# Two layers of linear attention and MLP on one core: another order for the first loads, two dummy matmuls less, and the instruction lists settled anew

## The chip, the core and the metric

The kernel runs on one core of a Trainium2 chip. A core has TensorE (PE) for matmuls, VectorE (DVE), ScalarE (ACT) and GpSimd (POOL) for elementwise work, and SyncE (SP), which only issues transfers. Each engine runs its own list of instructions strictly in order; semaphores order one engine against another. PSUM has eight banks, into which TensorE writes; a bank is free again when another engine has read it. The metric is the time of one execution in microseconds (us) on the device.

## The reference

Input x is 2048 tokens of 512 features in bf16. Four residual blocks follow one another: attention, MLP, attention, MLP, with the same weights in both layers.

```python
def _A_ref(x, wqkv, wo):                       # H = 32 heads of 16
    q, k, v = split_heads(x @ wqkv)
    phi = lambda t: jnp.where(t > 0, t + 1, jnp.exp(t)) + 1e-6
    pq, pk = phi(q), phi(k)
    kv = jnp.einsum("bhsd,bhse->bhde", pk, v)
    z = jnp.einsum("bhsd->bhd", pk)
    o = jnp.einsum("bhqd,bhde->bhqe", pq, kv) / (jnp.einsum("bhqd,bhd->bhq", pq, z)[..., None] + 1e-6)
    return merge_heads(o) @ wo
def _B_ref(x, w1, b1, w2, b2):                 # F = 1792
    h = _gelu(jnp.einsum("bsd,df->bsf", _layernorm(x), w1) + b1)
    return jnp.einsum("bsf,fd->bsd", h, w2) + b2
for _ in range(2):
    x = x + _A_ref(_layernorm(x), A_wqkv, A_wo)
    x = x + _B_ref(_layernorm(x), B_w1, B_b1, B_w2, B_b2)
```

The sums kv and z run over all tokens, so each attention block has a point at which every token's keys must be done before any output can start.

## The kernel before

The 2048 tokens are 16 tiles of 128 (numbered 0 to 15), in four chunks of four. Names in the kernel carry the layer and the tile or chunk: K0_3 is the key matmul of layer 0, tile 3; Q0_1_2 the query matmul of layer 0, chunk 1, part 2.

A tile of the first attention goes through these steps. VectorE takes its statistics (statsA0, line 773, and aggrA0, line 775), VectorE or POOL adds epsilon (vepsA0, line 780), POOL takes the power -1/2 (powA0, line 782), and VectorE normalizes (normA0, line 795); or POOL makes a bias (nmr, line 787) and ScalarE normalizes (line 790). Tile 3 alone has its statistics on ScalarE: a sum (line 764), a negation on POOL (negA0_3, line 766) and a sum of squares (line 768). Tiles 0 to 5 are then transposed on TensorE (PTA0, line 817) and copied out of PSUM by ScalarE (tcA0, line 827); the others are transposed by transfers that SP issues (TA0, line 804). K (line 866) multiplies a transposed tile by the key weights; ScalarE takes exp (line 837) and, for some, relu (line 848), and VectorE or POOL makes phi of it (min at lines 841 and 850, phik at lines 843 and 854). G (line 958) adds up the product of phi(k) with the normalized tile over all 16 tiles in four PSUM banks that stay held until G0_15; Z (line 941) adds up phi(k). Q (lines 883 and 896) makes the queries. After G0_15 and the Zs come kv (line 1008), its product with wo (line 1031), the denominators (D, line 1074, or per token on VectorE and POOL with TP transposes on SP, lines 1051 to 1063), and the attention output WO (line 1097). The MLP is W1 (line 1127), gelu on ScalarE (line 1132), and W2 (line 1163).

All order is written out by hand in one table, CONF. CONF["ORDER"] has one list of operation names for each engine; CONF["PLACES"] gives every buffer slot (PSUM banks, the 12 large SBUF slots t4, the small ones) the list of tiles that hold it one after the other; CONF["WAY"] names the engine of each operation that can run on more than one. Settled (line 105) takes these lists as they are, and assign_waits (line 186) adds semaphore waits for data and for slots that are still in use. An operation whose data is late therefore holds up everything behind it in its engine's list.

CONF["WARM"] gives two groups of dummy matmuls, warm0 and warm1 (line 747), on a constant; all write the bank "warm". CONF["LOADS"] lists the first transfers: name, queue, what, chunk, from and to tile of the chunk (or row block of the weights), and what it waits for. x0 and x1 are the tiles of chunk 0, wk0 and wk1 two halves of the key weights, xc1 to xc3 the other chunks, wq the query weights. The remaining weights (wv, wo, w1, w2) are issued by POOL after all transposes of the first attention (late, line 725). POOL also prepares constants: the identity (idp), a block mask (bdm0, bdm1, lines 729 and 732), eps6, and zeros for the bias transfer (b1z, line 723), behind which SP's b1 and its transpose Tb1 wait.

In ORDER, SP begins with x0, x1, wk0; ScalarE with wk1, xc1, xc3, sumA0_3, wq, sqA0_3, tcA0_0; TensorE with warm0, warm1, PTA0_0, PTA0_1, K0_0.

Of the kernel before, what the change touches and what calls it, by code (L numbers as in the profile page):

```python
# [185 lines left out]
def assign_waits(graph, order, sems, dma_sems):  # L186
# [10 lines left out]
    while len(done) < total:  # L197
        moved = False
        for e in ENGINES:
# [42 lines left out]
    WARM=[[512, 512, 512, 512, 512, 512, 512, 512, 512, 512, 512], [512, 512, 512, 512]],  # L242
    LOADS=[['x0', 'sp', 'x', 0, 0, 1, ''], ['x1', 'sp', 'x', 0, 1, 4, ''], ['wk0', 'sp', 'wk', 0, 0, 2, ''], ['wk1', 'act', 'wk', 0, 2, 4, 'ones'], ['xc1', 'act', 'x', 1, 0, 4, 'x0'], ['xc3', 'act', 'x', 3, 0, 4, ''], ['wq', 'act', 'wq', 0, 0, 4, ''], ['xc2', 'act', 'x', 2, 0, 4, '']],
    ORDER={
# [38 lines left out]
        "act":  # L283
# [321 lines left out]
def build_kernel(nc, A_x, A_wqkv, A_wo, B_x, B_w1, B_b1, B_w2, B_b2, out, conf=None, report=False):  # L605
# [5 lines left out]
    with ExitStack() as es:  # L611
# [131 lines left out]

        for n, cols in enumerate(cf["WARM"]):
            def warm(e, cols=cols):
# [584 lines left out]
```

## Time and profile before

| what | value |
|---|---|
| runs | 327.53, 329.68 and 484.78 us; median 329.68 |
| profiled execution: its own time | 327.5 us |
| its span, first to last instruction | 326.3 us |
| TensorE busy | 322.2 us in 1723 matmuls |
| VectorE, ScalarE, POOL busy | 211.0, 193.1, 152.5 us |
| x0, 128 KB: issue to landing | 2.4 us |
| x1, 384 KB: issue to landing | 3.1 us |
| wk0 and wk1, 256 KB each: issue to landing | 4.5 and 4.0 us |

The profile gives for one execution the busy time of each engine, the chain of work that ended last (each instruction followed back to what released it), groups of instructions by source line, a timeline, and busy times by stretch of the span. Times within it count from the first instruction. A busy TensorE is not TensorE at its peak: matmul ends are modelled, and the distance between two starts tells the rate. In a timeline line the start comes first, then the duration, engine, line, operation, output and inputs, and in brackets the idle time before it with what ended it.

### The profile page before, as it was taken

How to read it: one execution, taken by the hardware profiler on the slowest of the kernel's cores; microseconds unless marked ns; L12 is line 12 of the kernel's file. 1: busy time of each engine (PE TensorE's matmuls, PEld its weight loads, DVE VectorE, ACT ScalarE, POOL GpSimd, SP SyncE). 2: the span in 40 equal slices, each digit the busy share in tenths (PEclk: the TensorE clock that was granted, in tenths of full speed). 3: DMA queues.
4: the chain of work that ended last, by engine and by line, in shares of the span. 5: the costliest groups of instructions: out<-in, count | busy, mean ns of one | idle time of the engine just before them, and what ended most of it. 6: DMA issues, size and time to landing. Idle time of an engine off the chain costs nothing.

```text
span 326.3 us, 4763 instructions
## 1 busy us (share of the span) xinstructions
PE 322.2 (99%) x1723; PEld 159.3 (49%) x1723; DVE 211.0 (65%) x503; ACT 193.1 (59%) x334; POOL 152.5 (47%) x224
## 2 busy tenths in 40 slices
PE   8999999999999999999999999999999999999997
PEld 3444445576454444444444444458644444444444
DVE  5987679996938685142436899999989983300112
ACT  4988769797661416529673477969833454551600
POOL 5662548588663417300757434783856593100000
PEclk9999999999999999999999999999999999999999
DMA  7355753334012210331011110012034322200102
GB/s 266 120 83 97 219 189 104 105 64 68 16 32 50 54 26 3 80 64 34 0 32 33 34 32 0 19 32 50 17 82 94 69 48 66 64 0 2 64 0 80
DMA packets 46883, 20.37 MB, mean 62 GB/s; under 512 B 41932, under 2 KB 45388, under 8 KB 46860
## 3 DMA queue, kind: packets, MB, share of 16 engines
q1 hardware_dynamic: 44572, 13.00, 18.8%
q0 software_dynamic: 1056, 4.72, 4.5%
q10 hardware_dynamic: 1232, 2.36, 2.0%
q8 instruction: 13, 0.21, 0.3%
q14 instruction: 10, 0.08, 0.1%
HBM read 8.00 MB, written 2.10 MB: 31 GB/s over the span
## 4 chain that ended last, share of the span: by engine, by line
PE 97%; DVE 1%; ACT 1%; issue 0%
PE ps L1127 30%; PE ps L1163 29%; PE ps L1097 9%; PE ps L866 8%; PE ps L883 5%; PE ps L987 4%; PE ps L958 4%; PE ps L896 2%; PE ps L747 2%; PE ps L1150 1%; PE ps L1074 1%; PE ps L1008 1%; PE ps L1031 1%; PE ps L941 1%; PE ps L817 0%; DVE pkb L854 0%
## 5 line engine op out<-in xcount | busy, mean ns | idle before, releaser
L1132 ACT ACTIVATE gT<-ps,b1c 128x512 bf16<-128x512 f32 (+1 forms) x140 | 77.1, 600 | 65.3 <-PE ps L1127 65.0
L1127 PE MATMUL ps<-t,w 128*128 128x512 bf16 (+1 forms) x560 | 102.2, 336 | 0.0
L1163 PE MATMUL ps<-w,gT 128*128 128x512 bf16 x434 | 97.6, 379 | 0.0
L1127 PEld LDWEIGHTS ps<-t,w 128*128 128x128 bf16 x560 | 54.6, 98 | 43.7 <-ACT t L827 0.3
L1163 PEld LDWEIGHTS ps<-w,gT 128*128 128x128 bf16 x434 | 42.5, 98 | 50.4 <-DVE xsb L1169 0.2
L782 POOL TENSOR_TENSOR rstd<-veps,neghalf 128x1 f32<-128x1 f32 x64 | 37.9, 602 | 33.5 <-DVE veps L780 31.4
L837 ACT ACTIVATE eb<-ps 128x512 bf16<-128x512 f32 x64 | 37.4, 614 | 18.3 <-PE ps L866 10.5
L1173 DVE TENSOR_TENSOR outb<-ps,xsb 128x512 bf16<-128x512 f32 x15 | 10.1, 686 | 46.3 <-PE ps L1163 40.3
L773 DVE BATCH_NORM_STATS2 stats<-xsb 128x6 f32<-128x512 f32 x48 | 32.3, 678 | 0.4
L848 ACT ACTIVATE rb<-ps 128x512 bf16<-128x512 f32 x45 | 26.6, 617 | 9.2 <-PE ps L866 8.7
L866 PE MATMUL ps<-wqkv,t 128*128 128x512 bf16 x128 | 31.6, 379 | 0.1
L1097 PE MATMUL ps<-gtb,t 128*128 128x512 bf16 x128 | 31.2, 379 | 0.1
L850 DVE TENSOR_SCALAR eb<-eb 128x512 bf16<-128x512 bf16 x45 | 14.0, 321 | 21.1 <-ACT eb L837 21.1
L1113 POOL TENSOR_TENSOR xsb<-xsb,b2b 128x512 f32<-128x512 f32 x20 | 24.3, 1224 | 6.8 <-ACT yb L790 6.6
L790 ACT ACTIVATE yb<-xsb,nmr,rstd 128x512 bf16<-128x512 f32 x21 | 16.7, 812 | 14.2 <-POOL nmr L787 13.9
L780 POOL TENSOR_SCALAR veps<-mv 128x1 f32<-128x1 f32 x35 | 7.6, 217 | 30.8 <-DVE mv L775 28.1
L1063 POOL TENSOR_TENSOR t<-t,rr 128x512 bf16<-128x512 bf16 x14 | 15.5, 1114 | 13.6 <-DVE rr L1059 12.9
L795 DVE TENSOR_SCALAR yb<-xsb,mv,rstd 128x512 bf16<-128x512 f32 x27 | 16.1, 602 | 8.5 <-POOL rstd L782 8.3
L1051 POOL TENSOR_TENSOR lr<-t,zrow 128x512 f32<-128x512 bf16 x15 | 17.9, 1191 | 5.7 <-ACT zrow L971 4.2
L883 PE MATMUL ps<-wqkv,t 128*128 128x512 bf16 x80 | 19.9, 379 | 0.0
L1097 PEld LDWEIGHTS ps<-gtb,t 128*128 128x128 bf16 x128 | 12.3, 98 | 14.7 <-DVE rr L1059 0.6
L866 PEld LDWEIGHTS ps<-wqkv,t 128*128 128x128 bf16 x128 | 12.0, 98 | 14.9 <-ACT t L827 1.0
(97 smaller groups left out, 373.5 us busy)
## 6 DMA issues: line engine op xcount, KB each, us to landing
w<-in_B_w_dram POOLq DMA_DIRECT2D x4, 896.0 KB, 6.9
out_dram<-outb SPq DMA_DIRECT2D x15, 128.0 KB, 1.9
t<-in_A_x_dram ACTq DMA_DIRECT2D x3, 512.0 KB, 4.6
t<-yb SPq DMA_TRANSPOSE x56, 2.5
wqkv<-in_A_wqkv_dram ACTq DMA_DIRECT2D x1, 512.0 KB, 5.8
wqkv<-in_A_wqkv_dram POOLq DMA_DIRECT2D x1, 512.0 KB, 4.6
wo<-in_A_wo_dram POOLq DMA_DIRECT2D x1, 512.0 KB, 5.5
t<-in_A_x_dram SPq DMA_DIRECT2D x1, 384.0 KB, 3.1
```

The lines of the kernel that those rows point to most:

```text
L773: G.op("dve", lambda e: e.bn_stats(stats[:, s.slot, :], src()), 620, reads=src_keys, writes=[k + "s"], tiles=[s, *src_tiles], name=f"stats ...
L782: G.op("pool", lambda e: e.tensor_tensor(rstd[:, s.slot:s.slot + 1], veps[:, s.slot:s.slot + 1], neghalf[:], op=ALU.pow), 570, reads=[k + ...
L837: G.op("act", lambda e: e.activation(eb[:, et.slot, :], bank(bt), ACT.Exp), 478, reads=[src_key], writes=[f"e{tag}"], tiles=[bt, et], name ...
L848: G.op("act", lambda e: e.activation(rb[:, rt.slot, :], bank(bt), ACT.Relu), 478, reads=[src_key], writes=[f"r{tag}"], tiles=[bt, rt], nam ...
L866: ins = e.matmul(bank(b), lhsT=yTa(yT)[:, dt, k * P:(k + 1) * P], rhs=wqkv[:, dt, D:2 * D], start=(dt == 0), stop=(dt == DT - 1))
L883: ins = e.matmul(bank(b), lhsT=yTa(yT)[:, dt, k * P:(k + 1) * P], rhs=wqkv[:, dt, 0:D], start=(dt == 0), stop=(dt == DT - 1))
L1051: lambda e, r=r, tok=tok: e.tensor_tensor(lr[:, r.slot, :], tok(), zrow[:], op=ALU.mult), 1150 if on_pool else 600,
L1097: ins = e.matmul(bank(wb), lhsT=yTa(pq)[:, kt, k * P:(k + 1) * P], rhs=gtb[:, kt, :], start=(kt == 0), stop=(kt == DT - 1))
L1113: G.op("pool" if on_pool else "dve", lambda e: e.tensor_tensor(xsb[:, st, :], xsb[:, st, :], b2b[:], op=ALU.add), 1120 if on_pool else 600 ...
L1127: ins = e.matmul(bank(b, n), lhsT=w1[:, dt, ft * P:(ft + 1) * P], rhs=yTa(yT)[:, dt, k0 * P:k1 * P], start=(dt == 0), stop=(dt == DT - 1))
L1132: G.op("act", lambda e, ft=ft, b=b, k0=k0, k1=k1, n=n: e.activation(gT[:, g.slot, ft * 512 + k0 * P:ft * 512 + k1 * P], bank(b, n), ACT.Ge ...
L1163: ins = e.matmul(bank(b), lhsT=gT[:, g.slot, ft * 512 + k * P:ft * 512 + (k + 1) * P], rhs=w2[:, ft, :], start=(ft == 0), stop=(ft == FT - 1))
```

## The change

Only CONF changes; the functions stay as they are.

- WARM: warm1 has two dummies instead of four. In TensorE's list PTA0_0 now stands between warm0 and warm1.
- LOADS: x1, now tile 1 alone, is issued by ScalarE as its first instruction. The two halves of the key weights follow, wk0 as SP's second and wk1 as ScalarE's second, which no longer waits for the memset "ones". x2, tiles 2 and 3, is ScalarE's third. Then xc1 (still behind the landing of x0), xc3, wq and xc2, all ahead of ScalarE's first arithmetic.
- ORDER: all five lists are settled anew. PLACES follows them.
- WAY: 34 operations move from POOL to VectorE and 29 from VectorE to POOL (epsilons, denominator products pz and pr, bias additions b2, sums za). POOL's bdm0, bdm1, eps6 and b1z move from the start of its list to the place where the late weights are issued.

The diff, cut to its core (the lists that are left out change in the same way):

```diff
 CONF = dict(
-    WARM=[[512, 512, 512, 512, 512, 512, 512, 512, 512, 512, 512], [512, 512, 512, 512]],
-    LOADS=[['x0', 'sp', 'x', 0, 0, 1, ''], ['x1', 'sp', 'x', 0, 1, 4, ''], ['wk0', 'sp', 'wk', 0, 0, 2, ''], ['wk1', 'act', 'wk', 0, 2, 4, 'ones'], ['xc1', 'act', 'x', 1, 0, 4, 'x0'], ['xc3', 'act', 'x', 3, 0, 4, ''], ['wq', 'act', 'wq', 0, 0, 4, ''], ['xc2', 'act', 'x', 2, 0, 4, '']],
+    WARM=[[512, 512, 512, 512, 512, 512, 512, 512, 512, 512, 512], [512, 512]],
+    LOADS=[['x0', 'sp', 'x', 0, 0, 1, ''], ['x1', 'act', 'x', 0, 1, 2, ''], ['wk0', 'sp', 'wk', 0, 0, 2, ''], ['wk1', 'act', 'wk', 0, 2, 4, ''], ['x2', 'act', 'x', 0, 2, 4, ''], ['xc1', 'act', 'x', 1, 0, 4, 'x0'], ['xc3', 'act', 'x', 3, 0, 4, ''], ['wq', 'act', 'wq', 0, 0, 4, ''], ['xc2', 'act', 'x', 2, 0, 4, '']],
...
         "sp":
-            "x0 x1 wk0 TA0_7 TA0_6 TA0_8 TA0_14 TA0_15 TA0_13 TA0_12 b2 TA0_10 TA0_11 TA0_9 b1 Tb1 TB0_1 TB0_0
+            "x0 wk0 TA0_6 TA0_8 TA0_7 TA0_14 TA0_15 TA0_13 b2 TA0_12 TA0_10 TA0_11 TA0_9 b1 Tb1 TB0_1 TB0_0
...
         "pe":
-            "warm0 warm1 PTA0_0 PTA0_1 K0_0 PTA0_2 K0_1 PTA0_3 K0_2 PTA0_4 G0_0_0 K0_3 K0_4 Q0_0_0 G0_1_0 PTA0_5 Q0_0_1 K0_5
+            "warm0 PTA0_0 warm1 PTA0_1 K0_0 PTA0_2 K0_1 PTA0_3 K0_2 PTA0_4 G0_0_0 K0_3 K0_4 PTA0_5 G0_1_0 Q0_0_0 Q0_0_1
...
-            Q0_1_3 Q0_1_1 Q0_0_3 Q0_0_2 G0_8_0 Z0_3 Z0_2 G0_9_0 G0_10_0 D0_0_0
+            Q0_1_3 Q0_1_1 Q0_0_3 G0_8_0 Q0_0_2 Z0_3 Z0_2 G0_9_0 G0_10_0 D0_0_0
...
         "act":
-            "wk1 xc1 xc3 sumA0_3 wq sqA0_3 tcA0_0 xc2 tcA0_1 expk0_0 tcA0_2 reluk0_0 tcA0_3
+            "x1 wk1 x2 xc1 xc3 wq xc2 tcA0_0 sumA0_3 tcA0_1 sqA0_3 expk0_0 tcA0_2 reluk0_0 reluk0_1 expk0_1 tcA0_3
...
         "dve":
-            "ones statsA0_0 aggrA0_0 vepsA0_0 normA0_0 statsA0_1 aggrA0_1 vepsA0_1 statsA0_2 aggrA0_2 normA0_1 statsA0_4
-            aggrA0_4 normA0_2 statsA0_5 normA0_3 statsA0_7 mink0_0 normA0_4 phik0_0
+            "ones statsA0_0 aggrA0_0 statsA0_1 aggrA0_1 vepsA0_1 normA0_0 normA0_1 statsA0_2 aggrA0_2 vepsA0_2 statsA0_4
+            normA0_2 statsA0_6 aggrA0_4 mink0_0 normA0_3 statsA0_5 normA0_4 phik0_0
...
-            phik0_9 phik0_13 mink0_11 minq0_0_3 phik0_11 minq0_1_3 minq0_0_2 zs0_2 zs0_3 zb0
+            phik0_9 phik0_13 mink0_11 phik0_11 minq0_0_3 minq0_1_3 phiq0_1_3 zs0_2 zs0_3 zb0
...
         "pool":
-            "id0 eps6 bdm0 bdm1 neghalf id1 powA0_0 negA0_3 b1z powA0_1 vepsA0_2 powA0_2 vepsA0_3 powA0_3
+            "id0 id1 neghalf vepsA0_0 powA0_0 powA0_1 negA0_3 powA0_2 vepsA0_3 powA0_3
...
-            powA0_9 nmrA0_11 wv wo w1_0 w1_1 phik0_14 phiq0_1_1 w2_0
+            powA0_9 bdm0 eps6 wv bdm1 wo phik0_14 w1_0 phiq0_1_1 w1_1 pr0_0_2 w2_0 b1z
```

In layer 1 the new VectorE list has rec1_3_3 ahead of RB1_1 (before: behind RB1_2).

472 rows, old and new, of tables (ORDER, PLACES, WAY) are left out of this document.

## The prediction

> **What bounds the kernel now.** I read first the page's span, busy times and chain by engine, to learn whether there is anything to win outside TensorE.
>
> ```profile
> span 326.3 us, 4763 instructions
> ...
> PE 322.2 (99%) x1723; PEld 159.3 (49%) x1723; DVE 211.0 (65%) x503; ACT 193.1 (59%) x334; POOL 152.5 (47%) x224
> ...
> PE 97%; DVE 1%; ACT 1%; issue 0%
> ```
>
> TensorE stands idle 326.3 - 322.2 = 4.1 us in all. The change removes no real matmul. So its whole reach is two dummies and whatever part of the idle time is a wait, and I looked for those in the chain in order of time.
>
> ```profile
> 0.84 6.34 PE ps L747 x15
> 7.17 0.24 PE ps L817 x4
> 7.43 0.60 ACT t L827
> 8.09 1.04 PE ps L866 x4
> ...
> 38.54 0.60 ACT eb L837
> 39.16 0.29 DVE eb L841
> 39.45 0.34 DVE pkb L854
> 39.84 0.55 PE ps L941 x16
> ...
> 250.42 0.13 issue
> ```
>
> The reader sees 15 dummies (L747), then a short detour over ScalarE, then TensorE without a break except near 39 us and 250 us. A dummy takes 6.34 / 15 = 0.423 us, while real matmuls of the same width are 0.86 / 4 = 0.216 us apart: until about 6.8 us the array runs at half speed (the clock column says 1.00 throughout, and does not show this).
>
> Third, the busy time by stretch, for who paces TensorE behind the dummies:
>
> ```profile
> 7.00:9.00 2.00, 1.71 (x14) 0.88 (x13) 1.93 (x7) 1.18 (x2) 1.50 (x5) 1.00 1.02 382
> 9.00:11.00 2.00, 2.00 (x17) 1.14 (x16) 1.99 (x6) 1.84 (x4) 0.88 (x3) 1.00 0.96 319
> ...
> 35.00:40.00 5.00, 4.34 (x40) 2.09 (x38) 3.60 (x7) 3.22 (x7) 2.69 (x4) 1.00 0.99 295
> ```
>
> After the stretch and its length come the busy times of TensorE, its weight loads, VectorE, ScalarE and POOL. VectorE has 1.93 and 1.99 of 2.00; it is full from 5 to 20 us, so at the start it is as much the bound as TensorE. From 35 to 40 us nobody is full: there TensorE waits on a chain. Fourth, VectorE's own timeline:
>
> ```profile
> 4.99 0.41 DVE L795 TENSOR_SCALAR yb<-t,mv,rstd 128x512 bf16<-128x512 bf16 x1 [0.68 <-POOL rstd L782]
> 5.32 0.69 DVE L773 BATCH_NORM_STATS2 stats<-t 128x6 f32<-128x512 bf16 x1
> ...
> 7.14 0.38 DVE L795 TENSOR_SCALAR yb<-t,mv,rstd 128x512 bf16<-128x512 bf16 x1
> ...
> 8.34 0.38 DVE L795 TENSOR_SCALAR yb<-t,mv,rstd 128x512 bf16<-128x512 bf16 x1
> ...
> 39.16 0.29 DVE L841 TENSOR_SCALAR eb<-eb 128x512 bf16<-128x512 bf16 x1 [0.95 <-ACT eb L837]
> ```
>
> Tiles 0, 1 and 2 are normalized at 5.40, 7.52 and 8.72.
>
> **The dummies and the first tiles.** Two dummies less is 2 x 0.427 = 0.85 us off TensorE's list. What of it stays is a walk with the rows' durations (a VectorE instruction that does not read the one before it starts some 0.08 early). Tile 1 now has 128 KB of its own, first on ScalarE's queue. ScalarE issued at 1.49 in the middle of its table load (0.79 to 2.07), so the load does not hold it: I take issue at 0.85 and 2.4 us as for tile 0, landing 3.3; VectorE reaches it at 4.04. Were it issued only at 2.07, it would land at 4.46 and cost 0.4. VectorE: statistics of tile 0 at 3.21, of tile 1 at 4.04, normalize tile 0 at 5.1 (its rstd is ready at 5.05) and tile 1 at 5.84 to 6.24. TensorE: 11 dummies end at 5.53, the four transposes of tile 0 at half speed (0.107 each) end at 5.98, two dummies at 6.82, transposes of tile 1 at 7.05; tcA0_0 on ScalarE is over at 6.8, the key weights are there at 6.2 as before or sooner (the same 1 MB is in flight; its last part landed 4.5 us after its issue at 1.72; SP now issues its key weights at 1.26 and ScalarE its own no longer behind the ones at 1.49). So K0_0 starts at **7.05 instead of 8.09**, a whole microsecond early.
>
> What is late next is tile 2. Tiles 2 and 3 are now the last of that 1 MB, about 6.2 (4.4 before); statistics of tile 2 start at 6.2, before at 6.33. Tile 3's sum on ScalarE, at 4.42 before, now stands behind tcA0_0: 6.66 to 7.39. On POOL negA0_3 (0.26) waits for it until 7.47, and **powA0_2 is queued behind negA0_3**: 7.76 to 8.33. Tile 2 is normalized at 8.40 to 8.78, no sooner than before (8.72). K0_0 ends at 7.91 and TensorE waits 0.9. Then the same way tile 3 at 10.05 (9.64), tile 4 at 10.98 (10.76), phik0_0 at 11.31 (11.19), and G0_0_0 starts at 11.4, exactly as before. The same set of work up to Q0_0_1 ends at 16.8 against 16.93. So the start gives **-0.1**, of bounds -0.85 (no wait takes the place) and +0.7 (tiles 2 and 3 landing only at 7.5, when the load behind them did: issued 3.21, 4.3 us; tile 2 is then ready at 9.6 instead of 8.8). That load, tiles 4 to 7, is read at 7.5 as before.
>
> On the Trainium skill. The row: half speed lasted 6.0 us of unbroken dummies. "TensorE: Matmul & The Clock Gate", Part 1, says that the warm-up is about 3.4 us of sustained activity in a free-running window, not a number of matmuls. By it the opening stays where it is and the sum with it. Its Part 4 says that transposes do not count as busy in the same way; by that a window with tile 0's transposes in it may fail, and the opening come 3.4 us later, an estimate of +0.5 us from that page. The slower rival below is the same mechanism with its length from rows.
>
> **The wait near 39 us.** In the chain, phik0_11 (L854, 39.45) is followed by Z0_2 (L941). On VectorE mink0_11 is over at 38.21, but the list has minq0_0_3 before phik0_11, and that waits 0.95 us for an exponential of Q (L837). In the new list phik0_11 comes right behind mink0_11: 38.25 to 38.7. Z0_3 lets TensorE go at 39.02, so the gap of 39.84 - 39.02 goes: **-0.8**. Next is zb0 for D0_0_0; its chain starts from Z0_2 and moves with it, and VectorE has 1.4 of 5 us free. Bounds: -0.9 (a gap of 0.1 before Q0_0_2 goes too, which now stands behind G0_8_0) and 0.
>
> **The wait at 250 us.** WO1_15_0 waits for TP1_3_3, issued at 248.0 behind rec1_3_3 at 246.5, which stood behind RB1_2. Now rec1_3_3 stands ahead of RB1_1, some 5 us sooner: **-0.3**, bounds 0 and -0.3.
>
> **Costed at nothing.** 34 operations go from POOL to VectorE and 29 back. In 215 to 240 us VectorE is busy 23.6 of 25.0; four come (0.8 + 1.0 + 1.0 + 0.74), three go (3 x 0.74), a net +1.3 that fills it. Cover: W11_1 starts at 245.1, a microsecond after its last transpose; without it up to +1.3. POOL's bdm0, eps6 go ahead of wv, where it idles 6.3 us; bdm1 (0.85) and phik0_14 (1.17) ahead of w1_0, phiq0_1_1 ahead of w1_1: phiq0_1_1 ended at 45.5, so that load goes out 10 us later than at 35.8, lands by 56 at its former 10.9 us, and is read at 63.8. b1z goes behind w2_0 (about 48.5), and on SP b1, Tb1 and then TB0_1 wait behind it; b1 and Tb1 held SP for 2.8 us (31.87 to 34.61) and TB0_1 was issued at 58.98, so some 7 us cover them. The transposes TA0 on SP keep their 1.25 us pace; K0_9 had 0.3 us to spare.
>
> **Sum.** 327.5 (the profiled execution's own time, 326.3 span + 1.2) - 0.1 - 0.8 - 0.3 = **326.3 us**. The median of the runs, 329.68, lies 2.2 above the profiled one; a difference under 2% either way is about what a measurement of this kernel can tell from none.
>
> **Rivals.**
> - The 0.85 stays whole at the start: 325.5. For: K0_0 is 1.0 early. Against: VectorE and POOL are full there. 0.10.
> - The gap at 39 us only moves to the next link: 327.1. For: four PSUM banks feed that stage. 0.13.
> - VectorE becomes the bound in 215 to 240 us: +1.3, 327.6. Against: POOL's chain gets shorter by it. 0.11.
> - Not what it says: tile 1 leaves only after the table load: 326.7. Against: the issue at 1.49. 0.04.
> - **Slower:** half speed lasts on. Dense dummies took 6.0 us to end it; if the break at 5.5 starts the count anew with K0_0 at 7.05, it ends at 13.0. From 6.8 to 13.0 my walk does 5.1 us of full-speed matmuls; at half speed 3.1 are done: +2.0, **328.3**. It decides from the point where the lag passes 1.2, half speed until 11.6. Against: one 0.4 us break, which is not idle. 0.10.
> - Left: a larger stall in the re-laid lists, over 2%. 0.04.
>
> The forecast has 0.48, its own range 325.8 to 326.9. With the rivals, and 2 us between runs, the range is 325.2 to 329.0. Faster by over 2% would need more than all idle time and both dummies (0.01); slower by over 2% only the last case (0.04); within, 0.95.
>
> **What the new profile would show.** L747 x13 in two groups; first L866 near 7.05; TensorE waiting some 0.9 us for L795 before the third group of L817; L941 near 39 us without a gap, none at 250; span 325.1. I am wrong if L866 matmuls stand 0.43 apart behind 7 us, if L764 waits for its load beyond 6.7, or if TensorE's busy share falls under 98% anywhere behind 40 us.

## The result, and the profile after

The changed kernel takes 327.74 us (median of 20 runs, from 326.94) against 328.87 us (20 runs, from 327.53) of the kernel before: ratio **0.9965**, 95% interval 0.9949 to 0.9981. That is the same by 2%, and a small gain clear of noise. The forecast was 326.3.

The profiled execution of that comparison was a disturbed one of 1938 us, so the profile shown here is that of a repeat of the same kernel, a_again (own time 327.26 us). First its page: span, busy times, and the shares of the chain that ended last.

```profile
span 326.0 us, 4723 instructions
...
PE 318.9 (98%) x1691; PEld 158.5 (49%) x1721; DVE 214.1 (66%) x508; ACT 193.6 (59%) x334; POOL 143.7 (44%) x219
...
PE 79%; DVE 12%; ACT 3%; DMA 2%; POOL 1%; issue 1%; DVEq 0%
```

The span is only 0.3 us shorter than before. TensorE has 1721 weight loads but 1691 matmul records: 30 matmuls are missing in this trace, about one in 57, and each leaves a hole of exactly 0.216 us. Below, a **gap** is the distance between two matmul starts less the usual distance, with such holes taken out. TensorE's share of the chain fell from 97% to 79%. Up to 30 us the chain now runs through VectorE, ScalarE, POOL and transposes as well, and from 209 to 246 us through VectorE, up to the transpose for which TensorE waits at 248 us (below).

TensorE's timeline at the start of a_again (start, duration, engine, line, operation, operands, count, and in brackets the idle time with what ended it; line numbers are two lower than before):

```profile
5.74 0.40 PE L815 MATMUL ps<-idp,yb 128*128 128x128 bf16 x4 [0.91 <-DVE yb L793]
5.98 0.60 PE L745 MATMUL ps<-const-bfloat16-1.0 128*128 128x512 bf16 x2
6.60 0.40 PE L815 MATMUL ps<-idp,yb 128*128 128x128 bf16 x4
6.83 1.03 PE L864 MATMUL ps<-wqkv,t 128*128 128x512 bf16 x4
8.75 0.40 PE L815 MATMUL ps<-idp,yb 128*128 128x128 bf16 x4 [0.88 <-DVE yb L793]
...
11.42 0.81 PE L956 MATMUL ps<-pkb,yb 128*128 128x512 bf16 x3
```

K0_0 (L864) starts at 6.83 instead of 8.09. Then TensorE waits for tile 2's normalized rows, and G0_0_0 (L956) starts at 11.42, where it was 11.40. The early start is given back within 5 us.

The wait near 39 us is gone. POOL, VectorE and TensorE in a_again:

```profile
36.05 1.17 POOL L852 TENSOR_TENSOR pkb<-eb,rb 128x512 bf16<-128x512 bf16 x1
36.83 0.67 DVE L852 TENSOR_TENSOR pkb<-eb,rb 128x512 bf16<-128x512 bf16 x1
...
38.04 0.43 DVE L852 TENSOR_TENSOR pkb<-eb,rb 128x512 bf16<-128x512 bf16 x1
...
38.89 0.94 PE L939 MATMUL ps<-onesm,pkb 128*128 128x1 bf16 x32
```

All 32 small matmuls of Z0_3 and Z0_2 (L939) now run in one piece; before, Z0_2 came 0.80 us behind Z0_3. The third row is phik0_11. The first two rows, phik0_14 on POOL and phik0_13 on VectorE, are explained by the experiments.

But there are waits that the kernel before did not have. They are best read in a second repeat, a_again_2 (profiled at 327.83 us), whose trace has all matmul records. TensorE's waits in it from 20 to 31 us, and from 240 to 255 us (line, what it waited for, us in total, times, longest):

```profile
PE ps L864 <- DMA t<-yb: 0.4, 1, 0.4
```

```profile
PE ps L1095 <- DMA t<-t: 0.2, 1, 0.2
PE ps L1125 <- DMA t<-yb: 0.2, 1, 0.2
```

All three are waits for a transpose on SP's queue: tile 12's at 29 us, and two at 244 and 248. The view counts idle time from modelled ends and leaves out a fourth, at 22 us: K0_7 starts at 22.68, 0.13 us after tile 7's transpose has landed, as K0_12 starts 0.14 after tile 12's. By starts of matmuls the gaps of a_again are 0.30 us at 22.4 (K0_7, for tile 7), 0.26 at 29.4 (K0_12, for tile 12), 0.19 at 244.4 (W1 of chunk 1) and 0.35 at 248.0 (WO): **1.10 us** together. In a_again_2 they are 0.25, 0.57, 0.34 and 0.39.

Tile 7 is late because POOL takes the power -1/2 of its variance late. The row in the kernel before:

```profile
12.57 0.55 POOL L782 TENSOR_TENSOR rstd<-veps,neghalf 128x1 f32<-128x1 f32 x1
```

and in a_again, where it is the second of two:

```profile
16.55 1.18 POOL L780 TENSOR_TENSOR rstd<-veps,neghalf 128x1 f32<-128x1 f32 x2
```

So like for like, from one profiled execution to the other (327.5 to 327.26), the change is worth -0.24 us. Gone are 0.11 at the start, 0.80 at 39, 0.30 at 250, and 0.18 in two small gaps at 31.3 and 36.6. Come are the 1.10, and 0.14 at 80.4. That makes -0.15, within 0.1 us of what the two times say. This is one pair of executions: the fastest runs of the comparison differ by 0.59 us, and the medians by 1.13, because the profiled execution of the kernel before is one of its fastest.

### The profile page after: what moved, and what is told of

The parts are those of the page before. It is cut to its first block, busy times and chain, and to the rows that moved or that the text cites. A ratio compares the mean times of both kernels' runs of the same rounds, so it can differ in the third digit from the quotient of the medians.

```text
span 1937.5 us, 4723 instructions
## 1 busy us (share of the span) xinstructions
PE 1906.5 (98%) x1691; PEld 531.5 (27%) x1721; DVE 216.3 (11%) x508; ACT 199.5 (10%) x334; POOL 139.2 (7%) x219
## 4 chain that ended last, share of the span: by engine, by line
PE 98%; issue 1%; DVE 0%; ACT 0%; DVEq 0%
PE ps L1125 30%; PE ps L1161 29%; PE ps L1095 9%; PE ps L864 8%; PE ps L881 5%; PE ps L985 4%; PE ps L956 4%; PE ps L894 3%; PE ps L1148 1%; PE ps L745 1%; PE ps L1072 1%; PE ps L815 1%; PE ps L1006 1%; PE ps L1029 0%; PE ps L939 0%
## 5 line engine op out<-in xcount | busy, mean ns | idle before, releaser
L1125 PE MATMUL ps<-t,w 128*128 128x512 bf16 (+1 forms) x553 | 598.5, 1439 | 6.6 <-issue 5.6
L1161 PE MATMUL ps<-w,gT 128*128 128x512 bf16 x426 | 575.4, 1706 | 6.6 <-issue 5.6
L1125 PEld LDWEIGHTS ps<-t,w 128*128 128x128 bf16 x560 | 180.6, 322 | 421.1 <-issue 417.0
L1161 PEld LDWEIGHTS ps<-w,gT 128*128 128x128 bf16 x434 | 140.1, 323 | 426.2 <-issue 425.2
L1095 PE MATMUL ps<-gtb,t 128*128 128x512 bf16 x124 | 173.4, 1707 | 4.7 <-issue 4.7
L864 PE MATMUL ps<-wqkv,t 128*128 128x512 bf16 x123 | 172.3, 1708 | 4.6 <-issue 3.7
L881 PE MATMUL ps<-wqkv,t 128*128 128x512 bf16 x78 | 109.8, 1711 | 2.8 <-issue 2.8
L985 PE MATMUL ps<-pkb,yb 128*128 128x512 bf16 x64 | 88.2, 1705 | 0.9 <-DVE gtb L997 0.9
L956 PE MATMUL ps<-pkb,yb 128*128 128x512 bf16 x63 | 87.3, 1704 | 0.9 <-issue 0.9
L864 PEld LDWEIGHTS ps<-wqkv,t 128*128 128x128 bf16 x128 | 41.0, 324 | 117.7 <-issue 114.4
L894 PE MATMUL ps<-t,wqkv 128*128 128x512 bf16 x47 | 65.5, 1703 | 0.9 <-issue 0.9
L881 PEld LDWEIGHTS ps<-wqkv,t 128*128 128x128 bf16 x80 | 25.3, 318 | 72.6 <-issue 71.2
L985 PEld LDWEIGHTS ps<-pkb,yb 128*128 128x128 bf16 x64 | 20.4, 322 | 61.8 <-issue 60.8
L956 PEld LDWEIGHTS ps<-pkb,yb 128*128 128x128 bf16 x64 | 19.9, 311 | 58.2 <-issue 55.9
```

The costliest lines, as they stand in the source:

```text
L864: ins = e.matmul(bank(b), lhsT=yTa(yT)[:, dt, k * P:(k + 1) * P], rhs=wqkv[:, dt, D:2 * D], start=(dt == 0), stop=(dt == DT - 1))
L881: ins = e.matmul(bank(b), lhsT=yTa(yT)[:, dt, k * P:(k + 1) * P], rhs=wqkv[:, dt, 0:D], start=(dt == 0), stop=(dt == DT - 1))
L894: ins = e.matmul(bank(b), lhsT=wqkv[:, dt, kt * P:(kt + 1) * P], rhs=yTa(yT)[:, dt, :], start=(dt == 0), stop=(dt == DT - 1))
L956: ins = e.matmul(ps[:, gb.slot + dc, :], lhsT=yb[:, y.slot, dc * P:(dc + 1) * P], rhs=pkb[:, pk.slot, :], start=(st == 0), stop=(st == ST ...
L985: ins = e.matmul(bank(b), lhsT=yb[:, ys[k].slot, dc * P:(dc + 1) * P], rhs=pkb[:, pks[k].slot, :], start=(k == 0), stop=(k == 3))
L1095: ins = e.matmul(bank(wb), lhsT=yTa(pq)[:, kt, k * P:(k + 1) * P], rhs=gtb[:, kt, :], start=(kt == 0), stop=(kt == DT - 1))
```

## The experiments

### The changed kernel again, and its parts undone

**a_again** is the changed kernel as it is.

> The changed kernel as it is, profiled once more. The prediction's terms: K0_0 starts near 7.05 us (before 8.09), TensorE waits some 0.9 us for tile 2 behind it, G0_0_0 starts at 11.4 as before (start -0.1); no gap before Z0_2 near 39 us (-0.8); no gap at 250 us (-0.3); span 325.1, 1.2 us under the one profiled of before. Rival 1: the start keeps the 0.85 of the two dummies (G0_0_0 at 10.55 to 10.8) and the gap at 39 us only moves. Rival 2: the whole gain is one of the three places and the other two are as before. The ratio to before, 0.9965, should come again within 0.002.

327.54 us (12 runs, 327.11 to 328.41), ratio 0.9960 (0.9936 to 0.9983). The start went as the prediction walked it, each step within 0.25 us, and the gap at 39 us went. The gaps of 22 to 29 and 244 to 248 us are in no term of the sum.

**a_warm4** gives the second group its four dummies back.

```diff
-    WARM=[[512, 512, 512, 512, 512, 512, 512, 512, 512, 512, 512], [512, 512]],
+    WARM=[[512, 512, 512, 512, 512, 512, 512, 512, 512, 512, 512], [512, 512, 512, 512]],
```

> The changed kernel with four dummies in the second group again instead of two. If the wait for tile 2 eats what the two dummies save (my step), the time is that of the changed kernel within 0.2 us: the four end at 7.25, K0_0 at 8.3, and tile 2 is not there before 8.8. If the saving is real (rival), it is 0.85 us slower, ratio to before 0.999 instead of 0.9965.

327.89 us, ratio 0.9978 (0.9950 to 1.0006). K0_0 starts at 7.06 instead of 6.83, tile 2's transposes at 8.76 instead of 8.75, G0_0_0 at 11.42 as before. By the profile two dummies lie inside the wait for tile 2 and cost nothing; the medians (327.89 and 327.54) do not separate the two kernels. The profiled execution is 0.27 us longer than a_again's, and the difference arises at 29 us, where tile 12's transpose landed 0.34 later.

**a_pow2** puts tile 2's power ahead of tile 3's negation on POOL.

```diff
-            "id0 id1 neghalf vepsA0_0 powA0_0 powA0_1 negA0_3 powA0_2 vepsA0_3 powA0_3
+            "id0 id1 neghalf vepsA0_0 powA0_0 powA0_1 powA0_2 negA0_3 vepsA0_3 powA0_3
```

> The changed kernel with powA0_2 ahead of negA0_3 in POOL's list. My step says that tile 2 is held by that order alone: normA0_2 starts 0.3 us sooner (8.1 instead of 8.4), and what follows on VectorE with it; up to 0.3 us faster than the changed kernel, less what tile 3 loses because its negation is 0.6 us later. Rival: tile 2 waits for its load or its statistics, and nothing changes but tile 3, 0 to 0.3 us slower.

328.11 us, ratio 0.9981 (0.9962 to 1.0000). Inconclusive for the profile: in this execution tiles 2 and 3 landed at 6.60 instead of 6.11 and the next chunk at 7.86 instead of 7.37, tile 2 was normalized at 8.50 (8.28), tile 3 later still, and G0_0_0 came at 12.18. Nothing was won by it; whether the order or the late loads cost the 0.76 us is not told apart. There was little to win: in a_again tile 2's epsilon is over at 7.54 and its power starts at 7.68, and in a_pow2, with nothing between them, the power starts 0.08 behind the epsilon. The negation held it by some 0.06 us.

### What took the wait near 39 us away

**b_phi11** does in the kernel before what the prediction thought decisive: phik0_11 ahead of minq0_0_3.

```diff
-            "phik0_9 phik0_13 mink0_11 minq0_0_3 phik0_11 minq0_1_3
+            "phik0_9 phik0_13 mink0_11 phik0_11 minq0_0_3 minq0_1_3
```

> The kernel before with one edit: phik0_11 ahead of minq0_0_3 in VectorE's list. My step: the gap before Z0_2 at 39 us goes and the kernel is 0.8 us faster, ratio 0.9976. Rival: the next link (zb0, the exponentials of Q) takes the gap over, ratio 1.000.

328.89 us, ratio 0.9999 (0.9976 to 1.0023): nothing won. phik0_11 ran early, at 38.84, and yet TensorE's timeline has a gap of 0.63 us ahead of Z0_2:

```profile
39.23 0.54 PE L941 MATMUL ps<-onesm,pkb 128*128 128x1 bf16 x16
...
40.27 0.55 PE L941 MATMUL ps<-onesm,pkb 128*128 128x1 bf16 x16 [0.49 <-ACT eb L837]
```

Z0_2 now waits for an exponential on ScalarE: expq0_1_1, which still reads the PSUM bank that Z0_2 is to write. It had been only 0.17 us behind the first cause.

**a_phi11late** is the reverse, in the changed kernel.

```diff
-            "mink0_11 phik0_11 minq0_0_3 minq0_1_3 phiq0_1_3
+            "mink0_11 minq0_0_3 phik0_11 minq0_1_3 phiq0_1_3
```

> The changed kernel with phik0_11 back behind minq0_0_3 on VectorE. If the place of phik0_11 set the gap near 39 us (the prediction's step), the gap is back: Z0_2 starts 0.7 to 0.9 us behind the end of Z0_3. If ScalarE's new order took the gap away (expq0_0_3 and expq0_1_1 now ahead of reluq0_1_1, so minq0_0_3 has its data at 38.05 and the PSUM bank of Z0_2 is free by 39.0), the gap stays under 0.15 us; phik0_11 then runs 0.3 us later, at about 38.35.

328.13 us, one run. phik0_11 ran at 39.03, and there is no gap: VectorE and TensorE show

```profile
39.03 0.42 DVE L852 TENSOR_TENSOR pkb<-eb,rb 128x512 bf16<-128x512 bf16 x1
...
39.72 0.94 PE L939 MATMUL ps<-onesm,pkb 128*128 128x1 bf16 x32
```

TensorE came there 0.83 us later than in a_again, but phik0_11 was over 0.68 us before Z0_2 began. So its place is neither enough nor needed. Of the 0.87 us above a_again, 0.67 come from the new gaps, here 0.63 at 22.5, 0.60 at 29.9 and 0.54 at 245.2, each at a late transpose.

**b_exp** tries the rival, ScalarE's order, in the kernel before.

```diff
-            "reluq0_1_3 expq0_1_3 reluq0_1_1 expq0_0_3 expq0_1_1 expq0_0_2
+            "reluq0_1_3 expq0_1_3 expq0_0_3 expq0_1_1 reluq0_1_1 expq0_0_2
```

> The kernel before with one edit on ScalarE: reluq0_1_1 behind expq0_0_3 and expq0_1_1 instead of ahead of them. phik0_11 stays behind minq0_0_3. If ScalarE's order set the gap near 39 us, it shrinks from 0.80 to 0.0-0.25 us (expq0_0_3 about 1.0 sooner, near 37.5). If the place of phik0_11 set it, the gap stays at 0.7 to 0.9.

329.56 us, one run; the gap shrank to 0.63 only. That rival fell too: expq0_0_3 was not free to come early, since it waits 0.57 us until phik0_13 on VectorE gives its buffer back. (The long time is from elsewhere: the first loads landed up to 1.2 us later than in the first profile and G0_0_0 started at 11.94.) Both orders hang on **phik0_13**, and its row in the kernel before stands beside one of POOL:

```profile
36.55 1.17 POOL L854 TENSOR_TENSOR pkb<-eb,rb 128x512 bf16<-128x512 bf16 x1
36.76 1.25 DVE L854 TENSOR_TENSOR pkb<-eb,rb 128x512 bf16<-128x512 bf16 x1
```

VectorE's product takes 0.42 us elsewhere. Here it starts 0.2 us behind POOL's phik0_14 and ends 0.29 us behind it, as if it had got under way only when POOL was done. It is so in all seven profiles that have this order (1.24 or 1.25 us). In the changed kernel POOL starts 0.8 us ahead, and VectorE's row is 0.65 to 0.67 us, again ending 0.29 behind POOL's.

**b_phi14** moves POOL's operation alone: phik0_14 ahead of two loads. That is a piece of the change that the prediction priced at nothing.

```diff
-            "nmrA0_11 wv wo w1_0 w1_1 phik0_14 phiq0_1_1 w2_0
+            "nmrA0_11 wv wo phik0_14 w1_0 w1_1 phiq0_1_1 w2_0
```

> The kernel before with one edit on POOL: phik0_14 (a product of two 128x512 tiles, 1.17 us) ahead of the loads w1_0 and w1_1 instead of behind them. In all five profiles with the old list POOL starts it 0.2 us before VectorE's phik0_13, and that takes 1.25 us and ends 0.28 us behind POOL's; with the new list it takes 0.67, alone 0.43. Theory 'held by POOL': phik0_13 now takes 0.4 to 0.5 us, reluq0_1_1, expq0_0_3 and phik0_11 come 0.5 to 0.8 us sooner, and the gap ahead of Z0_2 near 39 us shrinks from 0.80 to 0.0-0.3 us with phik0_11 still behind minq0_0_3. Theory 'place of phik0_11' (the prediction): the gap stays 0.7 to 0.9 us, since minq0_0_3 still waits for an exponential that has its own times.

327.69 us, one run. POOL, VectorE and TensorE:

```profile
34.93 1.16 POOL L854 TENSOR_TENSOR pkb<-eb,rb 128x512 bf16<-128x512 bf16 x1
...
37.53 0.41 DVE L854 TENSOR_TENSOR pkb<-eb,rb 128x512 bf16<-128x512 bf16 x1
...
39.40 1.08 PE L941 MATMUL ps<-onesm,pkb 128*128 128x1 bf16 x32
39.46 0.42 DVE L854 TENSOR_TENSOR pkb<-eb,rb 128x512 bf16<-128x512 bf16 x1
```

phik0_13 takes 0.41 us, and the gap ahead of Z0_2 is 0.13 us, with phik0_11 (39.46) still behind minq0_0_3 and ScalarE's order as it was. So in the kernel before this is the cause of most of the gap ahead of Z0_2. It is not the whole stage: TensorE's gaps from 35 to 41 us come to 0.42 us here, 0.90 in the first profile and nothing in a_again, so the other new orders have a part in it. The gain does not show in the time because tile 15's transpose took 1.9 us longer in this execution, a gap of 0.89 us at 25.5. That is one execution, and no run puts phik0_14 back in the changed kernel.

### Why the profiled execution of the kernel before was a fast one

**b_again** is the kernel before once more.

> The kernel before, unchanged: one more profiled execution, because the sum started from one of 327.5 us that turned out to be the fastest end of 35 runs (median 329.0). Theory A, the loss of a typical execution is a race of small POOL instructions with VectorE: the epsilon of tile 15 on POOL (0.19 us where it started 0.01 us ahead of VectorE's normalize, 0.92 us where it started 0.2 us behind it) is long again, the normalized tile 8 and the transposes behind it are about 0.6 us late from 18 us on, and nothing else differs; the execution takes 328.0 to 328.3. Theory B, the loss is in the transfers: a load or a transpose lands later by 0.5 us or more, with an epsilon of 0.2. Theory C, it is spread or at the end: TensorE's gaps up to 300 us are those of the first profile within 0.3 us in all, and the time is still over 328.5.

328.24 us, in the range of theory A. The span is 0.73 us longer than in the first profile, but only about half of that is theory A's. TensorE has two gaps that the first profile does not have: 0.39 us at 20.6, a wait for an exponential on ScalarE behind the late bias, and 0.31 at 24.4, where tile 14's transpose landed. That transpose was issued 0.8 us late and then took 4.15 us instead of 3.60; b_loads has the same gap (0.32) with a short epsilon. POOL and VectorE of b_again:

```profile
16.83 0.92 POOL L780 TENSOR_SCALAR veps<-mv 128x1 f32<-128x1 f32 x1
```

```profile
16.63 0.41 DVE L795 TENSOR_SCALAR yb<-t,mv,rstd 128x512 bf16<-128x512 bf16 x1
16.95 0.75 DVE L854 TENSOR_TENSOR pkb<-eb,rb 128x512 bf16<-128x512 bf16 x2
```

and the same in the first profile of the kernel before:

```profile
16.54 0.19 POOL L780 TENSOR_SCALAR veps<-mv 128x1 f32<-128x1 f32 x1
```

```profile
16.55 0.41 DVE L795 TENSOR_SCALAR yb<-t,mv,rstd 128x512 bf16<-128x512 bf16 x1
```

The epsilon of 128x1 on POOL takes 0.19 us where it starts just ahead of VectorE's normalize, and 0.92 us here, where it starts 0.2 us behind it: it then ends as VectorE's run of three operations ends. The bias of tile 8 on POOL and the transposes from tile 8 on are late by it. It was held in b_again, b_exp and b_phi11, and not in the first profile, b_phi14 and b_loads. In the last two it also started 0.2 us behind and still took only 0.25 us, with the bias behind it at 0.58 instead of 0.27; so the start alone does not say when it is held, and what decides is not shown.

**b_veps15** takes that epsilon off POOL.

```diff
 dve:
-            "vepsA0_12 aggrA0_14 mink0_3 vepsA0_14 minq0_0_0
+            "vepsA0_12 aggrA0_14 mink0_3 vepsA0_14 vepsA0_15 minq0_0_0
 pool:
-            "powA0_6 powA0_12 vepsA0_15 nmrA0_8 powA0_14
+            "powA0_6 powA0_12 nmrA0_8 powA0_14
 WAY:
+        "vepsA0_15": "dve",
```

> The kernel before with one small operation moved: the epsilon of tile 15 (128x1) goes from POOL to VectorE, which costs VectorE some 0.07 us at 16 us. If a POOL instruction that starts just behind a VectorE one is held until VectorE's run of operations is over, and this one is held in most executions, the median falls by 0.4 to 0.6 us, to about 328.4, and the profile has the bias of tile 8 on POOL at 16.6 to 16.9. If it is held only now and then, or something else makes the typical execution slower than 327.5, the median stays at 328.9 to 329.1.

328.01 us against 329.07 by the medians, but the ratio is 0.9988 (0.9963 to 1.0013): not clear. It was run again.

> The kernel before with the epsilon of tile 15 on VectorE, once more, since 12 runs left the ratio at 0.9988 with 1 inside its interval while the medians lay 1.06 us apart. If POOL's held epsilon is what makes a typical execution of the kernel before slower than the profiled one, the median is again 0.6 to 1.1 us below that of before; if it is only a part of it beside late transfers, 0.2 to 0.6; if not, within 0.2.

328.36 us against 328.25, ratio 0.9998 (0.9971 to 1.0025): **nothing won**. Six of its 12 runs lie from 327.2 to 327.9, and six from 328.8 to 329.5. So the held epsilon is about half of what b_again lost, but it is not what separates the median from the fast profile. That part stays open. What the profiles of long executions show besides are late transfers, the clearest in b_two.

**b_two** has both small edits, phik0_14 ahead of the loads and the epsilon on VectorE.

> The kernel before with two small edits: phik0_14 ahead of w1_0 on POOL, and the epsilon of tile 15 on VectorE instead of POOL. If POOL and VectorE holding each other made both losses (0.73 us at 18 us in most executions, some 0.6 us at 39 us), the median is 327.6 to 328.0 against 329.0 of the kernel before, about that of the changed kernel (327.5 to 327.7), without its loads, dummies or order. If they did not, it is 328.6 to 329.1.

327.59 us (12 runs, 326.95 to 329.03), ratio 0.9972 (0.9949 to 0.9995). By the ratio, two moved instructions in the old kernel are worth about what the whole change is worth. As b_veps15 alone won nothing sure, most of this should be phik0_14's, but no repeated run has that edit alone. Its own profile does not settle it: there POOL's phik0_14 starts 0.2 us ahead of another operation of VectorE, a min, and holds that instead: it takes 1.12 us, against 0.71 in the first profile and 0.29 where POOL is idle.

```profile
36.42 1.17 POOL L854 TENSOR_TENSOR pkb<-eb,rb 128x512 bf16<-128x512 bf16 x1
36.62 1.12 DVE L841 TENSOR_SCALAR eb<-eb 128x512 bf16<-128x512 bf16 x1 [0.97 <-ACT eb L837]
```

TensorE's gaps from 35 to 41 us come to 0.66 us in it, against 0.90 in the first profile. The profiled execution was a long one, 328.66 us. Busy times by stretch around 20 us (stretch, length, then busy us of TensorE, its weight loads, VectorE, ScalarE, POOL), and TensorE's wait in it:

```profile
19.00:20.00 1.00, 0.88 (x4) 0.19 (x2) 1.00 (x4) 1.00 (x2) 0.00 (x0) 1.00 0.65 116
20.00:21.00 1.00, 0.00 (x0) 0.00 (x0) 1.00 (x6) 0.61 (x2) 0.19 (x1) 1.00 0.28 15
```

```profile
PE ps L866 <- DMA t<-yb: 1.3, 1, 1.3
```

TensorE does nothing for a whole microsecond. Tile 6's transpose, issued at 16.92, landed at 21.07: 4.14 us, where 2.58 is what it took in the first profile.

### The loads alone, and the new waits taken away

**b_loads** has the new first loads in the kernel before, everything else old.

```diff
 LOADS:
-    ['x1', 'sp', 'x', 0, 1, 4, ''], ['wk0', 'sp', 'wk', 0, 0, 2, ''], ['wk1', 'act', 'wk', 0, 2, 4, 'ones'],
+    ['x1', 'act', 'x', 0, 1, 2, ''], ['wk0', 'sp', 'wk', 0, 0, 2, ''], ['wk1', 'act', 'wk', 0, 2, 4, ''], ['x2', 'act', 'x', 0, 2, 4, ''],
 sp:
-            "x0 x1 wk0 TA0_7
+            "x0 wk0 TA0_7
 act:
-            "wk1 xc1 xc3 sumA0_3
+            "x1 wk1 x2 xc1 xc3 sumA0_3
```

> The kernel before with the new first loads alone: tile 1 first on ScalarE, key weights next on both queues, tiles 2 and 3 behind them; all other lists, the 15 dummies and the order of VectorE as before. The prediction's step: tile 1 lands near 3.6 us instead of 4.4 to 5.4, tiles 2 and 3 near 6.1, and as the order of VectorE does not change, K0_0 starts at 8.0 to 8.4 us and G0_0_0 at 11.2 to 11.7, as in the profiles of the kernel before (11.40, 11.52): nothing gained. The rival, that early loads alone shorten the start: G0_0_0 at 10.8 or sooner.

328.57 us, one run. Tile 1 landed at 3.56, tiles 2 and 3 at 6.13. TensorE:

```profile
8.40 0.40 PE L817 MATMUL ps<-idp,yb 128*128 128x128 bf16 x4 [2.19 <-DVE yb L795]
8.63 1.03 PE L866 MATMUL ps<-wqkv,t 128*128 128x512 bf16 x4
...
11.94 1.03 PE L958 MATMUL ps<-pkb,yb 128*128 128x512 bf16 x4
```

G0_0_0 starts at 11.94, half a microsecond later than in the first profile. Tile 3's sum on ScalarE starts at 6.16 instead of 4.42, POOL's negation behind it at 6.97, and tile 1's power, behind that in POOL's list, at 7.33 (6.49). So in this execution the early loads without the new lists won nothing and cost some 0.5 us, for a reason that the rows show. How much of it is the loads is not sure: the eight profiles with the old loads have G0_0_0 at 11.15 to 11.94.

**a_mend** takes on the waits that the change brought: tile 7's power, bias and normalization sooner; the load of the bias b2 behind the transposes; the output OD1 behind two more of them.

```diff
 sp:
-            TA0_13 b2 TA0_12 TA0_10 TA0_11 TA0_9 b1
+            TA0_13 TA0_12 TA0_10 TA0_11 TA0_9 b2 b1
-            TP1_3_3 OD1 TP1_2_1 TP1_2_0 OD2
+            TP1_3_3 TP1_2_1 TP1_2_0 OD1 OD2
 act:
-            expk0_4 reluq0_0_0 reluq0_0_1 expq0_0_1 normA0_7
+            expk0_4 reluq0_0_0 normA0_7 reluq0_0_1 expq0_0_1
 pool:
-            nmrA0_8 vepsA0_14 vepsA0_15 powA0_14 powA0_7 nmrA0_7
+            nmrA0_8 powA0_7 nmrA0_7 vepsA0_14 vepsA0_15 powA0_14
```

> The changed kernel with the three new waits in its profile taken on: powA0_7, nmrA0_7 and normA0_7 earlier (tile 7's transpose leaves about 1.1 us sooner than 19.6), b2's load behind the transpose TA0_9 instead of ahead of TA0_12, and the output OD1 behind TP1_2_0 instead of ahead of TP1_2_1. A transpose right behind a plain transfer landed 3.3 to 4.1 us after its issue in the profiles, others 2.4 to 2.6; without one in front, TA0_12 and TP1_2_1 should take 2.4 to 2.6. If these waits bound TensorE: the gaps at 22.4 (0.5), 29.4 (0.04 to 0.6) and 248 us (0.2) go, and the time is 326.4 to 326.9, 0.7 to 1.1 below the changed kernel. If ScalarE's own list bounds TensorE at 22 us (K0_7 also waits there for the exponential that frees its bank), 0.4 us of this is not gained: 326.9 to 327.4.

326.94 us (12 runs, 326.46 to 327.77), ratio **0.9942** (0.9920 to 0.9964) to the kernel before: below both kernels. Its profiled execution (327.16 us, all records) has, on TensorE,

```profile
22.30 0.54 PE L939 MATMUL ps<-onesm,pkb 128*128 128x1 bf16 x16
22.71 1.02 PE L864 MATMUL ps<-wqkv,t 128*128 128x512 bf16 x4
...
29.61 1.03 PE L864 MATMUL ps<-wqkv,t 128*128 128x512 bf16 x4
```

no gap at 22, none at 29 (tile 12's transpose took 2.40 instead of 3.68 us), none at 248. One is left at 244.4, 0.41 us, behind the transpose TB1_7. That execution is itself only 0.10 us shorter than a_again's, and K0_7 starts no sooner in it (22.71); the rest is in gaps of 0.19 at 19.3, 0.14 at 39 and 0.25 at 62.9, the last of which a_again_2 has too (0.23). a_mend_2 and a_again_2 put the two kernels side by side on one chip.

> The changed kernel with the three new waits taken on (tile 7's transpose sooner, b2 behind the transposes, OD1 behind TP1_2_0), once more, beside the changed kernel itself on the same chip. If the waits that the change brought ate most of what its sum had won, the median is 0.4 to 0.8 us below the changed kernel's. If 326.9 against 327.5 was chance between chips, the medians lie within 0.3 us.

> The changed kernel once more, as the partner of the run with its waits taken away: 327.4 to 327.8 by the earlier 12 and 20 runs, and 1.0 to 1.3 us below the kernel before.

326.89 us against 327.35: 0.46 us below, the ratios to the kernel before 0.9958 (0.9937 to 0.9978) and 0.9971 (0.9950 to 0.9992). Two pairs of 12 runs each agree, 0.60 (on two chips) and 0.46 us, though the intervals overlap. Not all of it held: in a_mend_2 tile 7's transpose, issued 0.9 us sooner, took 4.21 us and left a gap of 0.34 us at 22.6, and 0.45 us stood at 247.9. What is gone in both is the wait at 29 us: tile 12's transpose took 2.4 us in both, and 3.5 to 4.1 in all five profiles that have b2 ahead of it. The expectation's reason for OD1 was wrong: TP1_2_1 behind it took 2.42 us in a_again, no longer than others.

## Why the prediction was right or wrong

**Start, -0.1: right.** K0_0 at 6.83 (7.05 forecast), tile 2 on TensorE at 8.75 (8.8), G0_0_0 at 11.42 (11.4), G0_2_0 at 16.82 (16.8). The rival that 0.85 stays whole fell, and a_warm4 shows that the dummies are worth nothing there. That POOL's order holds tile 2 was nearly a tie (0.06 us, a_pow2's rows); its load landed at 6.11 and VectorE's statistics of tile 4 stood ahead of it as well. The -0.1 itself is less than the spread: Q0_0_1, the last of the same set of work, starts at 15.80 to 16.49 in the eight profiles with the old start and at 15.96 to 16.71 in the seven with the new one.

**Half speed until 13 us: did not come, and its row was a chance.** The 6.0 us of half speed in the profile before are the long end of a spread (below). All repeats of the changed kernel were at full speed before 6.3 us.

**39 us, -0.8: right size, wrong step.** The gap went, but not because phik0_11 moved (b_phi11 won nothing, a_phi11late lost nothing there). It went mainly because POOL's phik0_14 no longer starts just ahead of VectorE's phik0_13 (b_phi14: 0.80 to 0.13). That the size came out is luck. The prediction had that move under "Costed at nothing", and did not ask why the product phik0_13, 0.42 us elsewhere, stood with 1.18 us in the chain. Its rival "only moves to the next link" was the right reading of its own step: 0.17 us is what moving phik0_11 alone could win.

**250 us, -0.3: wrong.** rec1_3_3 came at 239.1 instead of 246.5 and the gap at 250 went, but 0.19 at 244.4 and 0.35 at 248.0 took its place, in transposes of the same queue: +0.24 instead of -0.3. The 0.19 goes with a packet of instructions rather than with the order: TB1_7 took 4.05 to 4.39 us in the five profiles of the changed kernel and its variants in which such a packet began 1.9 to 2.4 us after its issue (see the last section), and 2.4 us, with no gap there, in the other two.

**"Costed at nothing": this is the step that failed.** VectorE between 215 and 240 us was busy 24.65 of 25 us (24.9 forecast) and TensorE had no gap there, though the chain to the wait at 248 us runs through it; the late weights and b1 were covered as said. But "the transposes TA0 on SP keep their 1.25 us pace" looked at the pace and not at which tile leaves when. Tile 7's power went from 12.57 to 17.07 us on POOL, its transpose from 15.35 to 19.56; and b2 went ahead of tile 12's transpose, which landed at 29.73 instead of 27.95. These two cost 0.30 and 0.26 us in a_again, 0.25 and 0.57 in a_again_2. Tile 12's wait is the order's: without b2 ahead of it the transpose takes 2.4 us. Tile 7's seems to need bad luck as well: its transpose took 3.01 us with a packet of instructions in its way, and at 2.4 us it would have landed at 22.0, before K0_7 was due at 22.4 (an estimate from these rows). With 244 to 248 us the new waits come to 1.10 us, about what the sum (-1.2) misses the measured -0.24 by. a_mend, which takes them on, comes to 326.9, with its fastest run at 326.46: most of the way to 326.3.

**The base, 327.5: the other step that failed, too low for a median.** The sum stood on one profiled execution, which proved to be at the fast end of the runs (327.5 of 327.5 to 331.2, median 329.0 in 35). By the medians this term alone is off by 1.37 us (328.87), nearly all of the 1.44 by which 326.3 missed 327.74. The text gave that distance but did not move the forecast. Had it, the errors would have hidden each other: 328.9 - 1.2 = 327.7, the measured median, for wrong reasons. Why the medians differ by 1.13 us where the two profiled executions differ by 0.24 stays open. The runs also tell far less than the 2% that the text allows: the interval here is 0.9949 to 0.9981.

## What to carry to other kernels

When a list is settled anew, the cost is not in the pace of a queue but in the one operation that moved far back: look up, for every transfer, when the work ahead of it is now done and who reads it. A row that is three times as long as its like is a finding in itself; look at what the neighbour engine was doing. And a sum for a kernel that hangs on many small waits needs more than one profile of before, or a base taken from the runs.

## What the runs showed of the hardware

**POOL and VectorE hold each other, in both directions.** VectorE's product of two tiles: 0.41 us alone, 0.67 when POOL's began 0.8 us ahead, 1.25 when it began 0.2 ahead, in both cases ending 0.29 behind POOL's. The Trainium skill, "SBUF — State Buffer", section "Who interferes with whom", says that an operation of VectorE with two inputs in SBUF contends with one of POOL that reads SBUF, and that the order of issue decides who blocks. The rows of the product agree. A min of VectorE, with one tile as input, was held as well (1.12 us, b_two). POOL's epsilon took 0.19 us ahead of VectorE's run of operations, and of five that started 0.2 us behind it three took 0.92 and two 0.25; the order of starts does not tell these apart.

**A transpose takes longer with a packet of instructions in its flight.** The traces list, beside the data, DMA packets of 16 KB of kind "instruction", of 0.9 to 1.8 us each. In the 16 profiles 60 transposes had such a packet begin 0.3 to 1.9 us after their issue; 59 of them took over 2.85 us, up to 4.5, while the median of all 1216 transposes is 2.48. The later the packet began, the longer they took: 2.85 to 3.8 us with it up to 0.7 us after the issue, 3.8 to 4.5 with it 1.2 to 1.9 after. Packets are not the only cause: 68 other transposes took over 2.85 us, among them all 14 that stood right behind b2 (3.5 to 4.1). Which transpose is hit changes with the execution: at the first tiles it was TA0_14 in most profiles of the kernel before and its variants, TA0_15 in b_phi14 and b_veps15_2, TA0_6 in b_two (with the microsecond of idle TensorE shown above; the packet began 2.05 us after the issue there) and TA0_7 in the changed kernel. No run moved a packet by itself, so this is a coincidence in all profiles, not an experiment. The Trainium skill, "Runtime: NRT & Kernel Launch", section "Instruction fetch mechanics", has these 16 KiB blocks, fetched by each engine's own queue, and calls their cost mostly hidden; for the transposes here it was not.

**When the array comes to full speed is a matter of chance.** The dummies' distance fell from 0.43 to 0.22 us at 3.4 us in three profiles, at 6.8 in that of the kernel before, and in between in the others, with the same dummies from 0.84 us on. The Trainium skill, "TensorE: Matmul & The Clock Gate", Part 1, says that the window runs freely and is 3.4 us long, which fits this spread of 3.4 us; the half microsecond either way that it also gives is too little for these runs.
